# Sliding-window attention with a star-ReLU layer: attention times V in 64x64 tiles, grouped with the scores

## The chip, the cores and the metric

The kernel runs on one core of a Trainium2 chip. The metric is device time in microseconds (us), and the median of a kernel's runs is what counts. A core has TensorE (PE; its weight loads are shown as PEld), VectorE (DVE), ScalarE (ACT), GpSimd (POOL) and SyncE (SP), which issues most transfers. They run side by side and wait for one another by semaphores. TensorE reads SBUF and writes PSUM, which has eight banks of 2 KB in each of 128 partitions.

## The reference

Eight sequences of 576 tokens with 8 heads of 64 go through attention with a window of 32 tokens to either side, and then through a two-layer network.

```python
scores = scale * np.matmul(q, k.transpose(0, 1, 3, 2))       # q, k, v: (8, 8, 576, 64), float32
mask = np.abs(pos[:, None] - pos[None, :]) <= 32
scores = np.where(mask, scores, -1000000000.0)
scores = scores - np.max(scores, axis=-1, keepdims=True)
attn = np.exp(scores)
attn = attn / (np.sum(attn, axis=-1, keepdims=True) + 1e-09)
x = np.matmul(attn, v)                                       # -> 4608 tokens x 512
h = x @ w_in                                                 # 512 x 2048
r = np.maximum(h, 0.0)
g = s * (r * r) + b
out = g @ w_out                                              # 2048 x 512
```

## The kernel before

**Tiles.** The 4,608 tokens, all sequences end to end, are cut into 36 token tiles j of 128. A tile's queries are two halves u of 64. Half 0 sees the 128 keys that begin 32 tokens ahead of the tile, half 1 the 128 keys that begin 64 tokens later. So an attention tile needs 192 keys, which is why k and v are loaded shifted by 32 tokens: load j of k or v holds tokens 128j-32 to 128j+96, and tile j reads loads j and j+1.

**Attention of one tile (`attend`).** SyncE loads q, k and v in rows of 256 bytes (64 floats of a head). GpSimd casts them to bf16 (`KQN`, with k and q of a step side by side, and `VE` for v). `kq_turn` transposes k and q: up to step 11 by eight TensorE transposes into the bank TP and a copy (`kqt<-tp`), later by a DMA transpose. `scores` (line 761) is 24 matmuls in a 64x64 tiling, 16 of 64 columns and 8 of 128, into two banks SC, one for each head of a pair. For each head VectorE then adds the mask and takes the row maximum (line 773), and ScalarE takes the exponential and its row sum (line 781). VectorE inverts the sums, GpSimd multiplies (line 797). P is transposed, from tile 6 on by a DMA transpose (`pts<-p`). `av` (line 845) multiplies with v into the bank AV: 16 matmuls in a 128x64 tiling, 8 with `VE` for half 0 and 8 with `VO` for half 1. `VO` is v shifted by 64 rows, so that half 1's 128 keys stand in one tile of partitions: its two halves are cast by VectorE or ScalarE from two loads (`make_vo`, `vo<-v`). Tiles 0 to 3 use `VE` alone, in two steps and two tilings (`NSPLIT`), tiles 0 to 2 another form of attention altogether (`attend_light`). VectorE copies AV into `XT` (`xt<-av`).

**The two layers.** For a token tile (eight of 128 tokens, then fourteen of 256) the first layer (line 950) is blocks of eight or sixteen matmuls that fill one bank of 512 columns; the banks HT0 and HT1 and, from tile 11 on, TP take turns. ScalarE applies the relu (line 959), VectorE squares into `GT` (line 978). The second layer (line 998) goes by sub-tiles of 128 tokens: 16 matmuls of 512 columns, in four blocks of four, into the bank OUTP or PTP in turn. In the last three token tiles SC1 and AV join in. VectorE scales the bank, adds a constant (line 1012, `outs<-...`), and SyncE stores it.

**The order.** Nothing is ordered by hand. Every step is a node with an engine (or a choice of engines), a cost, a key, and the tiles it reads and writes. `_Plan.order` simulates the engines when the program is built: whichever engine is free first takes, of its nodes that are ready, the one with the smallest key. The result is a fixed instruction order for each engine. A key is about the token number at which the step is due: attention of tile j has 128j less 500 to 640, a first-layer block its token plus its share of the tile, a second-layer block one token tile later; relus, squares and evictions have lower keys. Two nodes that use the same bank or buffer are ordered by that. `PE_SLACK` lets TensorE plan with 400 ns more than the simulated end of another engine's step.

```python
            n = min(here, key=lambda m: (m.key, m.nid))                       # 144
            free[e] = t + n.cost                                              # 157
                    late = PE_SLACK if u.eng == "pe" and t > STEADY else 0.0   # 173
```

**Loads.** `FIRST` lists the loads of the start (K, Q: a whole sequence; i, o: quarters of the two weight matrices; k, q, v: single loads). Later ones come `AHEAD` = 4 tiles ahead, and behind the transposed P of five tiles back (`GATE`).

Of the kernel before, what the change touches and what calls it, by code (L numbers as in the profile page):

```python
# [6 lines left out]
F32 = mybir.dt.float32  # L7
# [18 lines left out]
PE_SLACK, STEADY = 400.0, 60000.0  # L26
FILL, FILL_MIN, FILL_SHARE, FILL_NS = ("attn", "ffn", "sums"), 300.0, 0.7, 115.0


class _Node:  # L30
# [4 lines left out]
                 "hard")  # L35

    def __init__(self, nid, eng, fn, cost, lat, key, dsem, ndma, dtime):
        self.nid = nid
        self.eng = eng
        self.fn = fn  # L40
        self.cost = cost
        self.lat = lat
        self.key = key
        self.deps = {}
        self.dsem = dsem
        self.ndma = ndma
        self.dtime = dtime
# [10 lines left out]
        self.hard = None  # L58


class _Plan:
# [39 lines left out]
    def order(self):  # L101
# [28 lines left out]
        while len(out) < len(self.nodes):  # L130
# [13 lines left out]
            n = min(here, key=lambda m: (m.key, m.nid))  # L144
            if isinstance(n.eng, tuple):
# [11 lines left out]
            free[e] = t + n.cost  # L157
            if n.dsem is None:
# [90 lines left out]
    stage = None  # L249


def bass_sliding_window_symmetric__then__act_starrelu_kernel(
# [20 lines left out]
    FINE, NFLEX, TAIL = 0, 6, 3  # L273
# [8 lines left out]
    NSPLIT, NWHOLE = 4, 0  # L282
# [14 lines left out]
    with ExitStack() as es:  # L297
# [10 lines left out]
        NL, NB, NVE, NVO, NKT, NP, NS, NPT, NG, NR1, NO, NM = 4, 4, 5, 4, 5, 4, 4, 3, 12, 4, 4, 4  # L308
# [4 lines left out]
        Q32 = [sb((128, DM), F32, "q32") for _ in range(NL)]  # L313
        K32 = [sb((128, DM), F32, "k32") for _ in range(NL + 1)]
        V32 = [sb((128, DM), F32, "v32") for _ in range(NL + 1)]
        KQN = [sb((128, 2 * DM), BF16, "kqn") for _ in range(NB)]
        VE = [sb((128, DM), BF16, "ve") for _ in range(NVE)]
        VO = [sb((128, DM), BF16, "vo") for _ in range(NVO)]
        KQT = [sb((128, 2 * NPAIR, 128), BF16, "kqt") for _ in range(NKT)]
# [145 lines left out]
        def parts(t0):  # L465
            got = []
            lo, hi = max(t0, 0), min(t0 + 128, T)
# [8 lines left out]
        def load(src, t0, dst, name, key, sem, x):  # L476
            pcs = parts(t0)

            def fn(e):
                return [e.dma_start(dst[r:r + n, :].rearrange("p (h d) -> p h d", h=H),  # L480
                                    src[b, :, s0:s0 + n, :].rearrange("h s d -> s h d"))
                        for (b, s0, r, n) in pcs]

            tot = sum(n for (_, _, _, n) in pcs)
            gate = turned.get(x - GATE)
            lastload[0] = add("sp", fn, 640.0 * len(pcs), key, writes=[name], dsem=sem,
                              ndma=len(pcs), dtime=1300.0 * tot / 128, behind=lastload[0],
                              ndesc=8 * tot, after=[gate] if gate and gate.eng == "pe" else [])
# [67 lines left out]

        def load_q(j):
            s_ = j % NL
            load(q, 128 * j, Q32[s_], ("Q32", s_), 128 * j - LEAD - 600, f"dq{s_}", j)

        def cast_q(j):
            s_, d_ = j % NL, (j + 1) % NB
            cast(CSET(j), Q32[s_][:, :], ("Q32", s_), KQN[d_][:, DM:2 * DM],
                 ("QN", d_), ckey("q", j, akey(j) - 200))

        def load_k(j):
            s_ = j % (NL + 1)
            load(k, 128 * j - 32, K32[s_], ("K32", s_), 128 * j - LEAD - 730, f"dk{s_}", j - 1)

        def cast_k(j):  # L570
            s_, d_ = j % (NL + 1), j % NB
            cast(CSET(j - 1), K32[s_][:, :], [("K32", s_)],
                 KQN[d_][:, 0:DM], ("KN", d_), ckey("k", j, akey(j) - 330))

        def load_v(j):
            s_ = j % (NL + 1)
            load(v, 128 * j - 32, V32[s_], ("V32", s_), 128 * j - LEAD - 729, f"dv{s_}", j - 1)
# [6 lines left out]
        def make_vo(j):  # L584
            s_, a, b_ = j % NVO, j % NVE, (j + 1) % NVE
            if j < NSPLIT:
                return
# [8 lines left out]
        def kq_turn(j, n0, n1):  # L596
            kn, kt = j % NB, j % NKT
            key = akey(j) - 128
            if j > KQDMA:
                add("sp", lambda e: [e.dma_start_transpose(KQT[kt][:, :, :], KQN[kn][:, :])],  # L600
                    1300, key + 64, reads=[("KN", kn), ("QN", kn)],
                    writes=[("KT", kt), ("QT", kt)], dsem=f"dkt{kt}", dtime=1600, ndesc=1024)
                return
            names = (["K"] if n0 == 0 else []) + (["Q"] if n1 == 8 else [])
# [6 lines left out]
            add("pe", fn, 60 * (n1 - n0), key, reads=[(x + "N", kn) for x in names] + ["IDENT"],  # L611
                writes=["TP"])
            move(FLEX(j - 1), {"dve": 80 + 76.0 * (n1 - n0), "act": 190 + 106.0 * (n1 - n0)},
                 KQT[kt][:, n0:n1, :], TP[:, n0:n1, :], key, ["TP"], [(x + "T", kt) for x in names])

# [125 lines left out]
        def attend(j):  # L741
            key = akey(j)
            ka, kb = j % NKT, (j + 1) % NKT
            ve, vo = j % NVE, j % NVO
# [5 lines left out]
            kq = turns if whole else [("QT", kb), ("KT", ka), ("KT", kb)]  # L750

            def scores(e):
                for pr in range(NPAIR):
                    for u, kt, x0, x1, y0 in ((0, ka, 0, 128, 0), (1, kb, 0, 64, 128), (1, ka, 64, 128, 64)):
                        for hh in range(2):
                            if whole:
                                qq, kk = qs(j, pr, hh, 64 * u, 64 * u + 64), keys(j, pr, hh, y0, y0 + x1 - x0)
                            else:
                                qq = KQT[kb][64 * hh:64 * hh + 64, NPAIR + pr, 64 * u:64 * u + 64]
                                kk = KQT[kt][64 * hh:64 * hh + 64, pr, x0:x1]  # L760
# [4 lines left out]
            add("pe", scores, 400, key, reads=kq, writes=[("SC", 0), ("SC", 1)])  # L765
# [20 lines left out]
            fine = j < FINE  # L786
            for c0, c1 in ((0, 4), (4, 8)) if fine else ((0, 8),):
                ys = range(c0, c1)
                add("dve", lambda e, c0=c0, c1=c1: e.tensor_scalar(
                    SM[mb][:, c0:c1], SM[mb][:, c0:c1], 1e-9, None, ALU.add),  # L790
                    150, key + 3, reads=[("SM", mb, y) for y in ys], writes=[("SE", mb, c0)])
                add("dve", lambda e, c0=c0, c1=c1: e.reciprocal(RC[mb][:, c0:c1], SM[mb][:, c0:c1]),  # L792
                    180, key + 3, reads=[("SE", mb, c0)] + [("SM", mb, y) for y in ys],
                    writes=[("RC", mb, y) for y in ys])
                for y0 in range(c0, c1, 4):
                    def norm(e, y0=y0):
                        return e.tensor_tensor(  # L797
                            P[pb][:, y0:y0 + 4, :], P[pb][:, y0:y0 + 4, :],
                            RC[mb][:, y0:y0 + 4].unsqueeze(2).broadcast_to([128, 4, 128]), ALU.mult)

                    cost = {"dve": 620.0, "pool": 1000.0}
                    eng = ("dve", "pool") if j < NDIV else "pool"
                    add(eng, norm if eng == "pool" else {x: norm for x in eng},
                        cost["pool"] if eng == "pool" else cost, key - 300,
                        reads=[("P", pb, y) for y in range(y0, y0 + 4)]
                        + [("RC", mb, y) for y in range(y0, y0 + 4)],
                        writes=[("P", pb, y) for y in range(y0, y0 + 4)])

            for part, (c0, c1) in enumerate(((0, 4), (4, 8)) if fine else ((0, 8),)):
                avp, ares = AV, "AV"  # L810
                if fine and part:
                    avp, ares = PTPF[:, :].rearrange("p (a b) -> p a b", b=128), "PTP"
                ptp = halves(PTPF if fine and part else AVF)

                if j >= PDMA:
                    turned[j] = add("sp", lambda e: [e.dma_start_transpose(
                        PTS[ptb][:, :, :], P[pb][:, :, :].rearrange("p a b -> p (a b)"))],
                        1300, key + 4, reads=[("P", pb, y) for y in range(8)],
                        writes=[("PTS", ptb, y) for y in range(8)], dsem=f"dpt{ptb}", dtime=1600, ndesc=1024)
                else:  # L820
                    def turn(e, c0=c0, c1=c1, ptp=ptp):
                        for y in range(c0, c1):
                            r = e.transpose(ptp[:, y, :], P[pb][:, y, :], IDENT[:, :])
                        return r

                    turned[j] = add("pe", turn, 59 * (c1 - c0), key + 4,
                        reads=[("P", pb, y) for y in range(c0, c1)] + ["IDENT"], writes=[ares])
# [251 lines left out]
```

## Time and profile before

| What | Value |
|---|---|
| median of three runs | 326.09 us (325.95 to 326.39) |
| the profiled execution | 325.7 us, span 323.9 us from first to last instruction |
| TensorE clock granted over the span | 0.995 |
| scores, 64x64, line 761 (tiles 4 to 35) | 768 matmuls |
| av, line 845 (tiles 3 to 35) | 280 matmuls from `VE`, 256 from `VO` |
| first layer, 256 columns | 896 matmuls, 273 ns each |
| second layer, 512 columns, OUTP and PTP | 467 matmuls recorded, 379 to 380 ns each |
| casts `vo<-v` | 49 on VectorE (552 ns), 15 on ScalarE (613 ns) |
| `xt<-av` on VectorE | 33 of 686 ns |
| evictions `outs` of 512 columns on VectorE | 744 to 748 ns |
| DMA | 173,121 packets, 61.56 MB, 163,728 packets under 512 bytes |

Matmuls are pipelined: a matmul's time in the profile runs from its start to its result, and the next one starts much earlier. What a block costs TensorE is read from the starts of the blocks. A few matmul records are missing, so a block of four may show as three.

### The profile page before, as it was taken

How to read it: one execution, taken by the hardware profiler on the slowest of the kernel's cores; microseconds unless marked ns; L12 is line 12 of the kernel's file. 1: busy time of each engine (PE TensorE's matmuls, PEld its weight loads, DVE VectorE, ACT ScalarE, POOL GpSimd, SP SyncE). 2: the span in 40 equal slices, each digit the busy share in tenths (PEclk: the TensorE clock that was granted, in tenths of full speed). 3: DMA queues.
4: the chain of work that ended last, by engine and by line, in shares of the span. 5: the costliest groups of instructions: out<-in, count | busy, mean ns of one | idle time of the engine just before them, and what ended most of it. 6: DMA issues, size and time to landing. Idle time of an engine off the chain costs nothing.

```text
span 323.9 us, 10043 instructions
## 1 busy us (share of the span) xinstructions
PE 310.7 (96%) x3877; PEld 214.9 (66%) x3925; DVE 236.1 (73%) x912; ACT 207.7 (64%) x715; POOL 164.6 (51%) x219
## 2 busy tenths in 40 slices
PE   6889989999999999999999999999999999999996
PEld 4557957766776757666675767575767666666664
DVE  2456886989987788894887787879867889843332
ACT  4414854688984859873769865779746778823330
POOL 5567589646767364655464564536671646410000
PEclk9799999999999999999999999999999999999999
DMA  5999879959999999999999999999999564420011
GB/s 168 340 300 263 293 254 233 234 128 232 204 176 212 203 208 191 231 186 241 183 237 215 211 229 219 210 220 213 201 223 215 125 140 99 98 67 34 32 64 68
DMA packets 173121, 61.56 MB, mean 190 GB/s; under 512 B 163728, under 2 KB 163984, under 8 KB 173072
## 3 DMA queue, kind: packets, MB, share of 16 engines
q1 hardware_dynamic: 172784, 60.90, 90.0%
q8 instruction: 31, 0.51, 0.7%
q14 instruction: 18, 0.15, 0.2%
q10 hardware_dynamic: 288, 0.00, 0.0%
HBM read 37.03 MB, written 9.44 MB: 143 GB/s over the span
## 4 chain that ended last, share of the span: by engine, by line
PE 85%; DVE 6%; ACT 3%; DMA 3%; issue 2%; POOL 0%; SPq 0%; POOLq 0%
PE ht L950 28%; PE outp L998 16%; PE ptp L998 15%; PE tp L950 8%; PE sc L761 3%; PE av L845 3%; DMA gt<-in_q_dram 3%; ACT p L781 2%; PE sc L998 2%; DVE gt L978 2%; PE av L998 2%; ACT r L959 1%; PE ht L431 1%; PE av L701 1%; PE tp L608 1%
## 5 line engine op out<-in xcount | busy, mean ns | idle before, releaser
L950 PE MATMUL ht<-xt,win 128*128 128x256 bf16 (+1 forms) x1152 | 113.7, 249 | 0.1
L781 ACT ACTIVATE p<-ss,mx 128x128 bf16<-128x128 f32 x264 | 102.5, 391 | 16.0 <-DVE mx L773 14.8
L978 DVE TENSOR_TENSOR gt<-r 128x512 bf16<-128x512 bf16 x144 | 78.2, 545 | 46.5 <-ACT r L959 45.2
L950 PEld LDWEIGHTS ht<-xt,win 128*128 128x128 bf16 x1152 | 91.2, 98 | 19.0 <-issue 0.3
L797 POOL TENSOR_TENSOR p<-p,rc 128x512 bf16<-128x512 bf16 x65 | 70.4, 1103 | 57.4 <-DVE rc L792 57.4
L959 ACT ACTIVATE r<-ht 128x512 bf16<-128x512 f32 x112 | 66.1, 592 | 44.7 <-PE ht L950 43.0
L998 PE MATMUL outp<-wout,gt 128*128 128x512 bf16 (+1 forms) x245 | 62.4, 373 | 2.5 <-issue 1.4
L773 DVE CUSTOM_DVE_ANT_0 ss<-sc,mask 128x128 f32<-128x128 f32 x264 | 61.5, 280 | 3.6 <-PE sc L761 3.3
L998 PE MATMUL ptp<-wout,gt 128*128 128x512 bf16 x238 | 61.5, 379 | 1.5 <-issue 0.6
L781 ACT ACTIVATION_READ_ACCUMULATOR p<-ss,mx 128x1 f32 x264 | 49.9, 189 | 0.0
L500 POOL CAST ve<-v 128x512 bf16<-128x512 f32 x37 | 24.9, 675 | 31.8 <-PE av L845 30.4
L998 PEld LDWEIGHTS ptp<-wout,gt 128*128 128x128 bf16 x256 | 24.0, 98 | 22.6
L998 PEld LDWEIGHTS outp<-wout,gt 128*128 128x128 bf16 x272 | 24.3, 98 | 18.6 <-DVE gt L978 0.2
L950 PE MATMUL tp<-xt,win 128*128 128x256 bf16 x256 | 33.2, 273 | 0.0
L959 ACT ACTIVATE r<-tp 128x512 bf16<-128x512 f32 x32 | 19.0, 595 | 20.1 <-PE tp L950 18.9
L500 POOL CAST kqn<-k 128x512 bf16<-128x512 f32 x33 | 22.4, 679 | 15.8 <-DMA k<-in_k_dram 15.8
L950 PEld LDWEIGHTS tp<-xt,win 128*128 128x128 bf16 x256 | 24.8, 98 | 6.1
L500 DVE CAST vo<-v 64x512 bf16<-64x512 f32 x49 | 27.1, 552 | 0.9
L500 DVE CAST xt<-av 128x512 bf16<-128x512 f32 x33 | 22.6, 686 | 6.0 <-PE av L845 5.8
L500 POOL CAST kqn<-q 128x512 bf16<-128x512 f32 x32 | 22.2, 693 | 2.2 <-DMA q<-in_q_dram 2.1
L773 DVE DVE_READ_ACCUMULATOR2_ANT mx<- 128x1 f32 x264 | 21.1, 80 | 0.0
L761 PEld LDWEIGHTS sc<-kqt 64*64 64x64 bf16 x768 | 10.7, 108 | 9.0 <-issue 6.8
(125 smaller groups left out, 255.1 us busy)
## 6 DMA issues: line engine op xcount, KB each, us to landing
out_dram<-outs SPq DMA_DIRECT2D x35, 256.0 KB, 3.1
v<-in_v_dram SPq DMA_DIRECT2D x28, 256.0 KB, 5.3
q<-in_q_dram SPq DMA_DIRECT2D x28, 256.0 KB, 4.4
k<-in_k_dram SPq DMA_DIRECT2D x25, 256.0 KB, 3.9
gt<-in_moe_w_in_dram SPq DMA_DIRECT2D x4, 1024.0 KB, 10.1
gt<-in_moe_w_out_dram SPq DMA_DIRECT2D x4, 1024.0 KB, 5.7
v<-in_v_dram SPq DMA_DIRECT2D x8, 192.0 KB, 4.6
k<-in_k_dram SPq DMA_DIRECT2D x7, 192.0 KB, 3.2
```

Of the source, the lines that this page charges most:

```text
L431: r = e.matmul((HT[1] if stage == "attn" else OUTP)[:, 0:256], lhsT=ONES[:, 0:128], rhs=ONES[:, :], start=True, stop=True)
L500: return e.tensor_copy(dst, src)
L608: r = e.transpose(TP[:, pr, :], KQN[kn][:, 128 * pr:128 * pr + 128], IDENT[:, :])
L761: r = e.matmul(SC[hh][64 * u:64 * u + 64, pr, x0:x1], lhsT=qq, rhs=kk, start=True, stop=True)
L773: lambda e, ss=ss, x=x, y=y, pr=pr, hh=hh: e.tensor_tensor_reduce(out=SS[ss][:, x, :], in0=SC[hh][:, pr, :], in1=MASK[kind][:, :], scale=- ...
L781: lambda e, ss=ss, x=x, y=y: e.activation(P[pb][:, y, :], SS[ss][:, x, :], AF.Exp, bias=MX[mb][:, y:y + 1], scale=-1.0, accum_out=SM[mb][: ...
L797: return e.tensor_tensor(P[pb][:, y0:y0 + 4, :], P[pb][:, y0:y0 + 4, :], RC[mb][:, y0:y0 + 4].unsqueeze(2).broadcast_to([128, 4, 128]), AL ...
L845: r = e.matmul(avp[64 * hh:64 * hh + 64, pr, 64 * u:64 * u + 64], lhsT=vt[k0:k1, d0:d0 + 64], rhs=PTS[ptb][k0:k1, 2 * pr + hh, 64 * u:64 * ...
L950: r = e.matmul(hbank[:, nt * f:nt * f + nt], lhsT=WIN[:, kc, 128 * ft:128 * ft + 128], rhs=XT[:, kc, x0:x0 + nt], start=(kc == 0), stop=(k ...
L959: return e.activation(R1[rb][:, :], hbank[:, :], AF.Relu, bias=0.0, scale=1.0)
L978: return e.tensor_tensor(d, r, r, ALU.mult)
L998: r = e.matmul(op_[:, 0:cn], lhsT=GT[:, g_, fc, :], rhs=WOUT[:, fc, c0:c0 + cn], start=(fc == 0), stop=(fc == 15))
```

## The change

1. **AV in 64x64 tiles.** From tile 6 (`NOLD`) on, AV is 24 matmuls. Eight take rows 64 to 127 of `VE[j]` (the 64 keys that all 128 queries of the tile use) with 128 columns into the bank PTP. Sixteen take rows 0 to 63 of `VE[j]` for half 0 and of `VE[j+1]` for half 1, with 64 columns, into the bank AV. ScalarE copies PTP into `HALF`, and VectorE adds AV and `HALF` into `XT`. `VO` is no longer made there. Tiles 3 to 5 use the old form with `VO`, in one group of 16.
2. **Grouping.** Nodes have a mode; `scores` and the new AV are "small". In the planner each change of mode on TensorE costs 97 ns (`CHANGE`). In small mode another ready small node is taken next, if its key is less than 800 (`HOLD`) above the one due. In full mode a single ready small node that is due is put off, as long as a full one is ready with a key less than 200 (`DEFER`) above.
3. **k in 512-byte rows.** k is loaded in chunks of 256 tokens, with two tokens in a partition (partition p has tokens 2p and 2p+1), which is 512 bytes in one piece. q keeps its rows and is put together in chunks of two tiles. k and q are cast, transposed and buffered apart, by chunks. The scores read the keys of a transposed chunk as pairs: a token of one plane, then one of the other, 1,024 bytes apart. `FIRST` has k2 for k4 and k5, and q5 ahead of v5.
4. **One output bank.** From token 640 (`ONE` = 5 tiles) on, up to the last three token tiles, all second-layer sub-tiles use OUTP, since PTP is AV's second bank.

```diff
+HOLD, DEFER, CHANGE = 800.0, 200.0, 97.0
...
             n = min(here, key=lambda m: (m.key, m.nid))
+            if e == "pe":
+                small = [m for m in here if m.mode == "small"]
+                if self.mode == "small" and n.mode != "small" and small:
+                    m = min(small, key=lambda m: (m.key, m.nid))
+                    if m.key < n.key + HOLD:
+                        n = m
+                elif self.mode != "small" and len(small) == 1 and n is small[0]:
+                    full = [m for m in here if m.mode != "small"]
+                    if full:
+                        m = min(full, key=lambda m: (m.key, m.nid))
+                        if m.key < n.key + DEFER:
+                            n = m
...
             free[e] = t + n.cost
+            if e == "pe":
+                if n.mode != self.mode:
+                    free[e] += CHANGE
+                self.mode = n.mode
...
-    FIRST = "K0 K1 Q0 Q1 v0 v1 i0 i1 i2 v2 v3 i3 v4 k4 k5 q4 o0 o1|v5 o2 o3||||"
+    FIRST = "K0 K1 Q0 Q1 v0 v1 i0 i1 i2 v2 v3 i3 v4 k2 q4 o0 o1|q5 v5 o2 o3||||"
...
+    AVK, NOLD, ONE, NVO = 5, 6, 5, 2
...
+        NR, NKT = {"k": 2, "q": 2}, {"k": 3, "q": 2}
...
+        def load_k(c):
+            s_ = c % NR["k"]
+            load("k", 256 * c - 32, 256, 2, R32["k"][s_], ("R32", "k", s_, 0), 2 * c - 1,
+                 256 * c - LEAD - 730, f"dk{s_}")
...
+        def cast_kq(x, c):
+            j = 2 * c - (x == "k")
+            src, dst = R32[x][c % NR[x]], KQN[x][c % NB]
+            if x == "k":
+                src = src[:, :].rearrange("p (h t d) -> p t h d", h=H, t=2)
+                dst = dst[:, :].rearrange("p (t h d) -> p t h d", h=H, t=2)
...
             if j > KQDMA:
-                add("sp", lambda e: [e.dma_start_transpose(KQT[kt][:, :, :], KQN[kn][:, :])],
+                add("sp", lambda e: [e.dma_start_transpose(flat, kn[:, :])],
...
             def fn(e):
-                for pr in range(n0, n1):
-                    r = e.transpose(TP[:, pr, :], KQN[kn][:, 128 * pr:128 * pr + 128], IDENT[:, :])
+                for i in range(8):
+                    r = e.transpose(TP[:, i, :], kn[:, 128 * i:128 * i + 128], IDENT[:, :])
                 return r
...
-                                kk = KQT[kt][64 * hh:64 * hh + 64, pr, x0:x1]
+                                rows, p0 = slice(64 * hh, 64 * hh + 64), 64 * (j % 2) + y0 // 2
+                                qq = KQT["q"][c % NKT["q"]][rows, j % 2, pr, 64 * u:64 * u + 64]
+                                kk = KQT["k"][(c + p0 // 128) % NKT["k"]][
+                                    rows, :, pr, p0 % 128:p0 % 128 + (x1 - x0) // 2].rearrange(
+                                    "q t p -> q p t")
...
-            add("pe", scores, 400, key, reads=kq, writes=[("SC", 0), ("SC", 1)])
+            add("pe", scores, 265, key, reads=kq, writes=[("SC", 0), ("SC", 1)]).mode = "small"
...
+            def av(e):
+                for pr in range(NPAIR):
+                    for hh in range(2):
+                        d0, y = 128 * pr + 64 * hh, 2 * pr + hh
+                        e.matmul(PTPF[64 * hh:64 * hh + 64, 128 * pr:128 * pr + 128],
+                                 lhsT=VE[ve][64:128, d0:d0 + 64], rhs=PTS[ptb][64:128, y, :],
+                                 start=(pr == 0), stop=(pr == NPAIR - 1))
+                    for u in range(2):
+                        for hh in range(2):
+                            d0, y = 128 * pr + 64 * hh, 2 * pr + hh
+                            r = e.matmul(AV[64 * hh:64 * hh + 64, pr, 64 * u:64 * u + 64],
+                                         lhsT=VE[(j + u) % NVE][0:64, d0:d0 + 64],
+                                         rhs=PTS[ptb][0:64, y, 64 * u:64 * u + 64],
+                                         start=(pr == 0 and u == 0),
+                                         stop=(pr == NPAIR - 1 and u == 1))
+                return r
+
+            add("pe", av, 265, key + AVK, reads=pts + [("VE", ve), ("VE", (j + 1) % NVE)], writes=["AV", "PTP"]).mode = "small"
+            hb = j % 2
+            add("act", lambda e: e.copy(HALF[hb][:, :], PTPF[:, :]), 620, key + AVK, reads=["PTP"],
+                writes=[("HALF", hb)])
+            add("dve", lambda e: e.tensor_tensor(
+                XT[:, :, 128 * (j % NX):128 * (j % NX) + 128], AV[:, :, :],
+                HALF[hb][:, :].rearrange("p (a b) -> p a b", b=128), ALU.add), 690, key + 5,
+                reads=["AV", ("HALF", hb)], writes=[("XT", j % NX, x) for x in range(2)])
...
-                                 )[ocnt[0] % (4 if last else 2)]
+                                 )[ocnt[0] % (4 if last else 2 if t0 < 128 * ONE else 1)]
```

More of the change, by code (lines that the diff above doesn't have):

```diff
@@ L58, in __init__ @@
         self.hard = None
+        self.mode = "full"
 class _Plan:
@@ L249 @@
     stage = None
+    mode = "full"
 def bass_sliding_window_symmetric__then__act_starrelu_kernel(
@@ new lines, in attend, with turn @@
+            pts = [("PTS", ptb, y) for y in range(8)]
+            if j >= PDMA:
+                turned[j] = add("sp", lambda e: [e.dma_start_transpose(
+                    PTS[ptb][:, :, :], P[pb][:, :, :].rearrange("p a b -> p (a b)"))],
+                    1300, key + 4, reads=[("P", pb, y) for y in range(8)],
+                    writes=pts, dsem=f"dpt{ptb}", dtime=1600, ndesc=1024)
+            else:
+                ptp = halves(AVF)
+                def turn(e):
+                    for y in range(8):
+                        r = e.transpose(ptp[:, y, :], P[pb][:, y, :], IDENT[:, :])
+                    return r
+                turned[j] = add("pe", turn, 472, key + 4,
+                    reads=[("P", pb, y) for y in range(8)] + ["IDENT"], writes=["AV"])
+                move(("act", "dve"), {"act": 1040.0, "dve": 810.0}, PTS[ptb][:, :, :], ptp, key + 4,
+                     ["AV"], pts)
@@ new lines, in attend, with av_one @@
+            if j < NOLD:
+                vo = j % NVO
+                def av_one(e):
+                    for u, vt in ((0, VE[ve]), (1, VO[vo])):
+                        for y in range(8):
+                            pr, hh = y // 2, y % 2
+                            r = e.matmul(AV[64 * hh:64 * hh + 64, pr, 64 * u:64 * u + 64],
+                                         lhsT=vt[:, 64 * y:64 * y + 64],
+                                         rhs=PTS[ptb][:, y, 64 * u:64 * u + 64],
+                                         start=(u == 0 and pr == 0), stop=(u == 1 and pr == 3))
+                    return r
+                add("pe", av_one, 460, key + AVK,
+                    reads=pts + [("VE", ve), ("VO", vo, 0), ("VO", vo, 64)], writes=["AV"])
+                add("dve", lambda e: e.tensor_copy(
+                    XT[:, :, 128 * (j % NX):128 * (j % NX) + 128], AV[:, :, :]), 690, key + 5,
+                    reads=["AV"], writes=[("XT", j % NX, x) for x in range(2)])
+                return
@@ L922, in attention_until @@
                 if NL <= x < NT:
-                    for what in (f"k{x + 1}", f"q{x}", f"v{x + 1}"):
+                    for what in ([f"k{x // 2 + 1}"] if x % 2 else []) + [f"q{x}", f"v{x + 1}"]:
                         if what not in place:
```

206 lines of the change are left out of this document (78 added, 128 removed).

## The prediction

> **What bounds the kernel now.** I read the page first: its busy times, its slices, then its chain of waits. Of this profiled execution (325.7 us, span 323.9 us) TensorE is busy 96%, and 85% of the chain that ended last runs through it.
>
> ```profile
> PE 310.7 (96%) x3877; PEld 214.9 (66%) x3925; DVE 236.1 (73%) x912; ACT 207.7 (64%) x715; POOL 164.6 (51%) x219
> PE   6889989999999999999999999999999999999996
> PE 85%; DVE 6%; ACT 3%; DMA 3%; issue 2%; POOL 0%; SPq 0%; POOLq 0%
> ```
>
> A busy share can hide stalls, so I asked next for TensorE's waits from 47 us to 320 us. No wait there is longer than 0.2 us, and those put down to "issue" are slots whose first matmul record is missing (three records of four). From 47 us on TensorE always has the next instruction, and what is taken from its stream comes off the end. The price of the pieces is read from the timeline of TensorE in a steady stretch (start, length, what):
>
> ```profile
> 158.23 1.03 PE L998 MATMUL outp<-wout,gt 128*128 128x512 bf16 x4
> 159.09 1.03 PE L998 MATMUL ptp<-wout,gt 128*128 128x512 bf16 x4
> 160.05 0.45 PE L761 MATMUL sc<-kqt 64*64 64x128 bf16 x24
> 160.43 1.04 PE L998 MATMUL outp<-wout,gt 128*128 128x512 bf16 x4
> 161.40 0.32 PE L845 MATMUL av<-pts,ve 128*64 128x64 bf16 x8
> ...
> 171.92 0.32 PE L845 MATMUL av<-pts,ve 128*64 128x64 bf16 x8
> 172.07 0.29 PE L845 MATMUL av<-pts,vo 128*64 128x64 bf16 x8
> 172.29 0.45 PE L761 MATMUL sc<-kqt 64*64 64x128 bf16 x24
> ```
>
> The reader is to look at starts. Four 512-wide matmuls take 158.23 to 159.09, 0.86 us. The four from 159.09 should end at 159.95; the scores start at 160.05: 0.10 us lost where the tiling goes from 128x128 to 64x64. The 24 score matmuls have all started 0.25 us later (0.45 less the 0.19 to 0.2 of the last), so they need 0.265 us, yet the next block starts only at 160.43, after 0.38. So a lone score block costs 0.48 us: 0.265 of work and 0.215 for the two changes of tiling. A lone AV block (16 matmuls of 128x64) costs 0.10 + 0.37 = 0.47. At 171.92 AV and scores adjoin, and one entry, 0.10, is saved; I count 5 such pairs among the 30 scores and 30 AVs of token tiles 6 to 35.
>
> **AV and grouping.** Before, those 60 blocks cost 30 x 0.48 + 30 x 0.47 - 5 x 0.10 = 28.0 us. After, AV is 24 matmuls in 64x64, eight of 128 columns and sixteen of 64, the same counts and widths as scores, on two banks as scores are. Nearest row: 0.265 us. From below, 512 columns on each of four quadrants, 0.216 us by the 512-wide matmul; from above, 24 at the old AV's 14 ns a start (8 starts in 0.10 to 0.12), 0.336. I take 0.265; the upper end adds 30 x 0.07 = 2.1 us. Each run of small blocks, however long, then costs 0.215 more: 60 x 0.265 + R x 0.215 = 15.9 + 0.215 R for R runs. All alone (R = 60): 28.8, 0.8 us worse. All paired (R = 30): 22.35. The planner holds a single ready small block back for up to 200 keys, at 128 keys per token tile and about 7.9 us a tile some 12 us; in the trace the next small block comes 1 to 7 us later. So pairs should be the rule, with singles where no full block is ready: R = 34, 23.2 us, **-4.8 us**.
>
> **Transposes by TensorE.** k and q are now turned in groups of eight for nine chunks up to tile 11: 72 instead of 60 (the row `tp<-ident,kqn` x60). Eight take 0.61 us less the last one's 0.22, so 56 ns each: **+0.7 us**, on the stall-free path.
>
> **The old AV of tiles 3 to 5.** Tile 3 loses its split (two groups, at 45.27 and 46.73, with a full block between): one entry and exit less and eight matmuls less, **-0.3 us**. It gains two half casts on VectorE or ScalarE (0.55, 0.61 us) ahead of it. TensorE waited 0.98 us there for VectorE's copy of P, so if the casts get in front of that, up to 1.1 us is lost; I take nothing, as they depend on loads only.
>
> **One output bank after token 640.** 25 sub-tiles of second-layer work (tiles 5 to 29) must wait for VectorE to empty the bank before. From the end of the issue of the last matmul: 0.16 us of pipeline, a median wait of 0.15, the eviction's 0.745, some 0.1 for the semaphore: 1.15 us, at worst (VectorE was late by 1.0 to 1.2 three times) about 2.2. It is hidden by first-layer blocks of 0.87 us, two of which are enough, and three banks feed them; before, bursts of three are common. Floor 0, ceiling 25 x 1.15 = 29 us. Near the floor, since first-layer work equals second-layer work and can run ahead: five evictions uncovered by 0.16, **+0.8 us**.
>
> **Beside the path.** ScalarE gains 30 copies PTP to HALF (the relu row of the same shape: 0.595 each, 17.9 us) and loses up to 15 V casts (9.2); it was busy 70 to 74% of 100 to 290 us. VectorE loses most of 49 V casts of 0.552 (27.1 us); its xt copy (0.686) becomes an add, 0.692 by the `xn` row. But this add now waits for ScalarE's HALF, and behind it in VectorE's queue stand squares, score reductions and the output evictions. TensorE hides that as long as the bank's 1.15 us is hidden. GpSimd casts the same elements. SyncE issues one k load where there were two, and 24 turns of k and q instead of 25; k's packets double from 256 to 512 bytes and halve in number. 2,048 packets go, 1,024 stay, so k's packet time cannot rise if a packet less than doubles; 256-byte packets took some 23 ns each in the trace, 2,048-byte ones about 95. In the start list k2 stands for k4 and k5, and q5 passes v5, o2 and o3: a shorter k against one more load, within 1 us either way, taken as nothing.
>
> **Scores from paired k rows.** k's turned chunk holds even tokens in one plane and odd ones in another, so scores stream their moving operand from two places 1,024 bytes apart in turn. No row shows TensorE reading so. ScalarE's `kwt<-tp` copies out of PSUM step 1,024 bytes and take 586 to 591 ns, against 592 for a plain relu, so stepping cost nothing there. Below: nothing (a gain is excluded, the columns are the same). Above: half rate, 0.216 us more a block. I take nothing, the nearest row.
>
> [...]
>
> **Sum.** -4.8 + 0.7 - 0.3 + 0.8 = -3.6 us: 322.1 for the profiled execution, whose 325.7 lies 0.4 under the median of 326.1; against that median, **322.5 us**. Its own range: R from 30 to 42 (-0.9, +1.7), bank 0 to 1.6, start +-1: 319.8 to 325.4.
>
> **Rivals.** *Slower by the strided k.* If the stream halves, 32 score blocks (tiles 4 to 35) cost 0.216 more: +6.9, 329.4 us. It decides above 3.6 / 32 = 0.11 us a block. For it: nothing in the trace excludes it. Against: the PSUM row. 0.17.
> *The single bank.* If the planner cannot place two first-layer blocks after each sub-tile, or the add on VectorE holds evictions back, each of 25 costs up to 1.15. At a third of that, +8.8 more: 331; from 0.18 us a sub-tile the gain is gone. Against: squares and relus kept three banks turning without a stall. 0.09.
> *Grouping does not happen.* R near 55, as with 5 pairs now: 15.9 + 11.8 = 27.7, so -0.3 + 0.7 - 0.3 + 0.8: 327.0, just slower. 0.05.
> *More than pairs.* With P turned early, runs of three: R = 22, -7.4, and the start a little shorter by VectorE's relief: 318.5. 0.09.
> *The forecast:* 0.60.
>
> **Numbers.** A measurement can tell about 0.2%, 0.65 us, from no change. Faster: forecast 0.58 of its 0.60, runs of three 0.09, and the mild ends of the bank and the strided k, 0.04: 0.71. Same 0.05, slower 0.24. Range 318.5 to 329.4: it reaches runs of three and the strided k; the bank's bad end stays out.
>
> **What would show it.** Right: in TensorE's timeline AV as `64*64 x24` beside scores, about 34 runs after 62 us, 0.265 us from a block's first start to the next block's, one exit of 0.115 a run; no TensorE wait on `outs` over 0.2 us; `half<-ptp` about 0.6. Wrong: score blocks of 0.48 inside (strided k); gaps ahead of `outp` released by VectorE (one bank); lone AV blocks (no grouping); waits on DMA or SP before 62 us (start list).

## The result, and the profile after

The changed kernel takes **330.96 us** (median of four runs, 330.83 to 332.44), the kernel before 326.02 (325.88 to 326.39) beside it: a ratio of 1.016 (95% interval 1.013 to 1.019). It is slower by some 5 us, where 3.6 us less was forecast, and it lies just above the range. The profiled execution took 331.0 us, 5.3 more than that of before; its span is 329.3 us. Medians and ranges here leave out executions with a lower granted clock that came out over 1.5% above the fastest of their kernel.

The page of the changed kernel, in the parts that were shown of before:

```profile
PE 314.1 (95%) x4119; PEld 220.5 (67%) x4169; DVE 219.6 (67%) x869; ACT 215.9 (66%) x731; POOL 163.1 (50%) x220
PE   6889999999999999999999999999999999999996
PE 79%; DMA 9%; DVE 3%; POOL 3%; issue 3%; SPq 2%; POOLq 0%
...
L901 ACT COPY half<-ptp 128x512 f32<-128x512 f32 x30 | 17.4, 579 | 10.5 <-PE av L892 10.5
...
L903 DVE TENSOR_TENSOR xt<-av,half 128x512 bf16<-128x512 f32 x30 | 20.5, 683 | 1.1 <-ACT half L901 1.1
```

TensorE is as busy as before in every slice, and VectorE has lost 16 us of work. So the 5 us are no new idle time in the middle of the kernel. TensorE's waits from 47 to 324 us (us in total, times, longest) say the same; those put down to "issue" are again slots whose first record is missing:

```profile
PE outp L1040 <- issue: 4.0, 25, 0.2
PE ht L992 <- DVE xt L903: 0.4, 1, 0.4
PE tp L929 <- DVE clo L925: 0.2, 1, 0.2
PE ptp L886 <- DMA pts<-p: 0.2, 1, 0.2
```

No wait on `outs` is left, and hardly one of any kind. The work itself takes longer. TensorE's timeline (start, length, what) shows which, in three places: scores alone, AV alone, AV and scores together.

```profile
126.96 1.04 PE L992 MATMUL ht<-xt,win 128*128 128x256 bf16 x8
127.93 0.69 PE L798 MATMUL sc<-kt,qt 64*64 64x128 bf16 x24
128.55 0.61 PE L1040 MATMUL outp<-wout,gt 128*128 128x512 bf16 x2
...
153.57 0.24 PE L886 MATMUL ptp<-pts,ve 64*64 64x128 bf16 x2
153.58 0.25 PE L892 MATMUL av<-pts,ve 64*64 64x64 bf16 x4
...
153.95 1.04 PE L1040 MATMUL outp<-wout,gt 128*128 128x512 bf16 x4
...
213.46 0.24 PE L886 MATMUL ptp<-pts,ve 64*64 64x128 bf16 x2
...
213.74 0.66 PE L798 MATMUL sc<-kt,qt 64*64 64x128 bf16 x22
214.33 1.05 PE L992 MATMUL ht<-xt,win 128*128 128x256 bf16 x8
```

The reader is to compare starts again. Scores alone hold TensorE from 127.93 to 128.55, **0.62 us, where they held it 0.38 before**. The new AV, with the same counts and widths in the same tiling, takes 153.57 to 153.95, 0.38. The pair takes 0.87. The entry (127.93 less 126.96 and 0.87) is 0.10, as before. To the nanosecond, a score block alone has grown from 0.377 to 0.620 us, by 0.243. The two kinds of block differ in what they stream: AV reads P in one piece, the scores read k as pairs from two planes.

### The profile page after: what moved, and what is told of

The parts are those of the page before. It is cut to its first block, busy times and chain, and to the rows that moved or that the text cites. A ratio compares the mean times of both kernels' runs of the same rounds, so it can differ in the third digit from the quotient of the medians.

```text
span 329.3 us, 10479 instructions
## 1 busy us (share of the span) xinstructions
PE 314.1 (95%) x4119; PEld 220.5 (67%) x4169; DVE 219.6 (67%) x869; ACT 215.9 (66%) x731; POOL 163.1 (50%) x220
## 4 chain that ended last, share of the span: by engine, by line
PE 79%; DMA 9%; DVE 3%; POOL 3%; issue 3%; SPq 2%; POOLq 0%
PE outp L1040 26%; PE ht L992 25%; PE tp L992 8%; PE sc L798 5%; DMA gt<-in_q_dram 3%; DMA v<-in_v_dram 2%; PE sc L1040 2%; DMA pts<-p 2%; DMA r32k<-in_k_dram 2%; PE ptp L886 2%; PE ptp L1040 2%; PE av L1040 2%; DVE gt L1020 1%; SPq L506 1%; POOL p L831 1%
## 5 line engine op out<-in xcount | busy, mean ns | idle before, releaser
L1020 DVE TENSOR_TENSOR gt<-r 128x512 bf16<-128x512 bf16 x144 | 82.4, 574 | 54.8 <-ACT r L1001 53.5
L1040 PE MATMUL outp<-wout,gt 128*128 128x512 bf16 (+1 forms) x436 | 111.9, 375 | 5.1 <-issue 4.1
L1040 PEld LDWEIGHTS outp<-wout,gt 128*128 128x128 bf16 x480 | 43.4, 98 | 33.8 <-issue 0.4
L526 POOL CAST kn<-r32k 128x512 bf16<-128x512 f32 x34 | 21.5, 659 | 7.3 <-DMA r32k<-in_k_dram 7.3
L1054 DVE SCALAR_TENSOR_TENSOR outs<-outp,scb,cvec 128x512 f32<-128x512 f32 (+1 forms) x30 | 22.1, 736 | 3.4 <-PE outp L1040 3.4
L901 ACT COPY half<-ptp 128x512 f32<-128x512 f32 x30 | 17.4, 579 | 10.5 <-PE av L892 10.5
L526 POOL CAST qn<-r32q 128x512 bf16<-128x512 f32 x32 | 20.1, 628 | 4.2 <-DMA r32q<-in_q_dram 4.2
L798 PE MATMUL sc<-kt,qt 64*64 64x64 bf16 (+1 forms) x768 | 22.1, 243 | 0.0
L903 DVE TENSOR_TENSOR xt<-av,half 128x512 bf16<-128x512 f32 x30 | 20.5, 683 | 1.1 <-ACT half L901 1.1
L798 PEld LDWEIGHTS sc<-kt,qt 64*64 64x64 bf16 x768 | 17.5, 107 | 4.7 <-issue 3.6
```

Of the source, the lines that this page charges most:

```text
L526: return e.tensor_copy(dst, src)
L798: r = e.matmul(SC[hh][64 * u:64 * u + 64, pr, x0:x1], lhsT=qq, rhs=kk, start=True, stop=True)
L901: add("act", lambda e: e.copy(HALF[hb][:, :], PTPF[:, :]), 620, key + AVK, reads=["PTP"], writes=[("HALF", hb)])
L903: add("dve", lambda e: e.tensor_tensor(XT[:, :, 128 * (j % NX):128 * (j % NX) + 128], AV[:, :, :], HALF[hb][:, :].rearrange("p (a b) -> p ...
L1020: return e.tensor_tensor(d, r, r, ALU.mult)
L1040: r = e.matmul(op_[:, 0:cn], lhsT=GT[:, g_, fc, :], rhs=WOUT[:, fc, c0:c0 + cn], start=(fc == 0), stop=(fc == 15))
```

## The experiments

The expectations name theories by letters. S is that the strided read of k is what costs; B is that the cause lies around the score blocks, above all in the single output bank. W, L, P, C and H are explained where they come.

**The strided read alone, in the kernel before.** Two planes of the buffer that holds k and q take turns, for tiles 5 to 35, and the scores also wait for the second plane; nothing else changes. What it computes are no longer the reference's scores.

```diff
-                                kk = KQT[kt][64 * hh:64 * hh + 64, pr, x0:x1]
+                                n, g = (x1 - x0) // 2, RUN[j % 4]                    # RUN = (1, 1, 1, 1)
+                                kk = (... if j == WHOLE else
+                                      KQT[kt][64 * hh:64 * hh + 64, pr:pr + 5:4, x0 // 2:x0 // 2 + n].rearrange(
+                                          "q t (p g) -> q p t g", g=g))
```

> The kernel before, and only the moving operand of its scores changed: from tile 5 on it is read as pairs from two places 1,024 bytes apart (one element of the k plane, one of the q plane, so the scores are not those of the reference). Theory S (the strided read alone makes the score blocks longer): a block's last matmul starts 0.47 us after its first instead of 0.25, the block takes 0.63 instead of 0.38, and 31 blocks give +7.8 us: 333.8. Theory B (the blocks of the changed kernel are long because of what stands around them, such as the single output bank or the AV in the same tiling): unchanged, 326.0, blocks of 0.38.

Measured: 333.81 us (333.73 to 334.23) against 326.02, ratio 1.0236 (1.0222 to 1.0249), +7.8. The timeline of this kernel:

```profile
157.26 0.69 PE L765 MATMUL sc<-kqt 64*64 64x128 bf16 x24
157.88 1.05 PE L954 MATMUL ht<-xt,win 128*128 128x256 bf16 x8
```

The block is the same 0.62 us long, and from 47 to 324 us TensorE shows no wait over 0.15 us. Theory S holds, size and place: 31 blocks of 0.243 are 7.5. There is neither a single output bank nor a new AV in this kernel, so theory B falls as the cause of the long blocks.

**How long a run must be.** The same edit, with 1, 2, 4 and 8 elements in one piece before the plane changes, by tile.

```diff
-    RUN = (1, 1, 1, 1)
+    RUN = (1, 2, 4, 8)
```

> The same as the strided kernel before, but the length of the runs that are read in one piece is 1, 2, 4 and 8 elements by tile modulo 4 (the scores are not those of the reference). Theory S in its form 'a single element at each place is what costs': 0.63 us for runs of one and 0.38 for runs of two, four and eight; about 328. In its form 'each change of place costs': 0.63, 0.50, 0.44, 0.41; about 329.7. Theory B: all 0.38, 326.

Measured once: 328.17 us. Its timeline has the four kinds in turn, 1, 2, 4, 8:

```profile
132.73 0.69 PE L765 MATMUL sc<-kqt 64*64 64x128 bf16 x24
133.35 1.04 PE L1002 MATMUL outp<-wout,gt 128*128 128x512 bf16 x4
...
140.01 0.47 PE L765 MATMUL sc<-kqt 64*64 64x128 bf16 x24
140.42 1.05 PE L954 MATMUL ht<-xt,win 128*128 128x256 bf16 x8
...
154.51 0.45 PE L765 MATMUL sc<-kqt 64*64 64x128 bf16 x24
154.89 1.05 PE L954 MATMUL ht<-xt,win 128*128 128x256 bf16 x8
...
161.55 0.45 PE L765 MATMUL sc<-kqt 64*64 64x128 bf16 x24
161.93 1.04 PE L1002 MATMUL outp<-wout,gt 128*128 128x512 bf16 x4
```

0.62, 0.41, 0.38, 0.38 us. Only a single element at each place comes near to halving the rate (first to last start 0.467 us against 0.252); two in a piece nearly restore it (0.276), four do. The distance between the planes is the same in all, so it is the run that counts. Of the two forms of theory S the first, that a single element is what costs, is right but for this small price of pairs, which took a tenth longer than runs of four.

**One output bank alone, in the kernel before.**

```diff
-                                 )[ocnt[0] % (4 if last else 2)]
+                                 )[ocnt[0] % (4 if last else 2 if t0 < 640 else 1)]
```

> The kernel before, with one output bank from token 640 on as in the changed kernel. Theory S: the bank costs no more than the few waits seen after the change, 326 to 327. Theory B: the bank costs what the change lost, 329 to 331, with gaps ahead of the second-layer blocks released by VectorE.

Measured: 329.24 us (328.31 to 329.52), ratio 1.0088 (1.0073 to 1.0103), +3.2. TensorE's waits, 47 to 324 us, of this kernel:

```profile
PE outp L998 <- DVE outs L1012: 2.0, 2, 1.2
PE ht L950 <- DVE mx L773: 0.3, 1, 0.3
```

Two waits for an eviction, at 101 and 119 us, are 2.0 of the 3.2. The time is theory B's, and yet this is not what slowed the changed kernel, whose own waits show no eviction at all. Its order is another one. That its slower scores leave VectorE more room is not the reason: repaired, with quick scores and the one bank, it shows no wait for an eviction either (two experiments on).

**The change with k loaded as before**, in two loads of 128 tokens, so that a plane holds tokens in order and the scores read in one piece.

```diff
-            load("k", 256 * c - 32, 256, 2, R32["k"][s_], ("R32", "k", s_, 0), 2 * c - 1, ...
+            for t in range(2):
+                if 256 * c - 32 + 128 * t < T:
+                    load("k", 256 * c - 32 + 128 * t, 128, 1, R32["k"][s_][:, DM * t:DM * t + DM], ...
...
-                                    rows, :, pr, p0 % 128:p0 % 128 + (x1 - x0) // 2].rearrange("q t p -> q p t")
+                                    rows, p0 % 256 // 128, pr, p0 % 128:p0 % 128 + x1 - x0]
```

> The changed kernel, with k loaded in 256-byte rows, a chunk as two planes of 128 tokens in order, so that scores read their keys in one piece; grouping, AV in 64x64 and the one bank stay. Theory S: score blocks of 0.38, 32 x 0.25 us less: 323.0. Theory B: 330 to 331. If k's 512-byte rows are needed for the transfers to keep up: score blocks of 0.38, but waits on DMA, 325 or more.

Measured: 327.51 us (325.99 to 328.42), ratio 1.004 (1.0023 to 1.0057). The blocks are back at 0.252 us first to last start, but the time is 4.5 above theory S. In this order there are 48 runs of small blocks instead of 40 (1.7 us), and TensorE waits 1.0 us once for the transposed P. It waits nowhere for k, so the longer rows were not needed for the transfers to keep up.

**The change with k in 512-byte rows but read in runs of 32.** The scores come out with a block's even tokens ahead of its odd ones; the masks are permuted to match, and ScalarE writes its exponentials back in the old order.

```diff
-                                    "q t p -> q p t")
+                                    "q t (b p) -> q b t p", p=32)
...
-                            P[pb][:, y, :], SS[ss][:, x, :], AF.Exp, bias=MX[mb][:, y:y + 1],
+                            P[pb][:, y, :].rearrange("q (b p t) -> q b t p", b=2, t=2),
+                            SS[ss][:, x, :].rearrange("q (b t p) -> q b t p", b=2, t=2), AF.Exp, ...
```

> The changed kernel with its 512-byte k rows, but scores read their keys in runs of 32 (even tokens, then odd tokens of a block of 64), with the mask in that order; ScalarE writes the exponentials back in token order. TensorE's order has the same 40 runs of small blocks. Theory S (the strided read is the loss, all else near the forecast): score blocks of 0.252 from first to last start, 32 x 0.25 = 8.0 us less: 323.0. Theory W (the order and its waits, above all of the one bank, are a second loss of some us, as the kernel before with one bank was 3.2 us slower): 324.5 to 326. If ScalarE's scattered write costs, its exponentials are over 0.39 us.

Measured: 326.01 us (324.39 to 327.09), ratio 0.9995 (0.9977 to 1.0014). The pair of AV and scores now takes 0.63 us instead of 0.87, and the number of runs is 40 as in the change:

```profile
134.92 0.24 PE L896 MATMUL ptp<-pts,ve 64*64 64x128 bf16 x2
...
135.55 1.04 PE L1050 MATMUL outp<-wout,gt 128*128 128x512 bf16 x4
```

But 5.0 of the 7.8 us came back, not all: the time is at the upper end of theory W. TensorE's waits of this kernel, 47 to 324 us:

```profile
PE ptp L896 <- DMA pts<-p: 0.9, 2, 0.5
PE ht L1002 <- DVE xt L913: 0.8, 2, 0.5
PE sc L804 <- DMA qt<-qn: 0.6, 1, 0.6
PE tp L939 <- DVE clo L935: 0.2, 1, 0.2
```

They are 2.5 us, against 0.8 (without the "issue" ones) in the change. TensorE, faster, has caught up with what feeds it: transposed P, q, and `XT`. None of the waits is for an eviction from the one bank, which theory W had named first. ScalarE's strided write has its price too, in the page's row of exponentials (0.429 us against 0.392):

```profile
L825 ACT ACTIVATE p<-ss,mx 128x128 bf16<-128x128 f32 x264 | 107.4, 429 | 13.9 <-DVE mx L816 13.5
```

**The same without the grouping.**

```diff
-            if e == "pe":        # the block that prefers or puts off a small node
+            if False:
```

> The same, without the planner's HOLD and DEFER rules (the price of a change of tiling stays): 56 runs of small blocks instead of 40. Theory 'a run costs 0.215': 16 x 0.215 = 3.4 us slower than with grouping. Rival (grouping also delays blocks, which costs as much): the same time within 1 us.

Measured: 330.26 us (329.57 to 333.55), ratio 1.015 (1.0112 to 1.0188), 4.25 above the kernel with grouping, with 56 runs instead of 40. Sixteen runs by 0.215 would be 3.4. TensorE's waits are 4.2 us here (among them 1.4 for a cast of q) against 2.5 with grouping, and may be the rest. The grouping gains about what the forecast's price of a run says.

**The same with two output banks throughout** (`ONE` = 99, so sub-tiles and AV share PTP).

```diff
-    AVK, NOLD, ONE, NVO = 5, 6, 5, 2
+    AVK, NOLD, ONE, NVO = 5, 6, 99, 2
```

> As e5, but second-layer sub-tiles keep taking OUTP and PTP in turn, so that AV and the second layer share PTP; the planner then puts small blocks together by three and four, 23 runs. Theory W: 17 runs less at 0.215 and the waits on the one bank gone, -3.7 to -5 against e5. Rival (AV waits for PTP to be emptied, and attention falls behind): slower than e5, with TensorE idle ahead of AV or of first-layer blocks that wait for xt.

Measured: 400.17 us, ratio 1.2265 (1.2243 to 1.2287). Only 23 runs are left, but the bank is now the bound. The largest of TensorE's waits, 47 to 324 us:

```profile
PE ptp L896 <- DVE xt L913: 14.6, 9, 2.2
PE ht L1002 <- DVE xt L913: 10.9, 7, 2.0
```

AV waits until the tile before has left the banks, and the first layer then waits for `XT`. The granted clock over the span was 0.919, against 0.995 before, so part of the loss is a slower TensorE (last section). AV's second bank can't be shared with the outputs in this way.

**The same, holding a single small block back longer.**

```diff
-HOLD, DEFER, CHANGE = 800.0, 200.0, 97.0
+HOLD, DEFER, CHANGE = 800.0, 800.0, 97.0
```

> As e5, with DEFER 800 instead of 200: a lone small block is held back longer, 36 runs instead of 40. Theory 'a run costs 0.215': -0.9 us against e5. Rival (held blocks come late): the same or slower, with waits on xt.

Measured: 334.15 us (331.82 to 334.67), ratio 1.0232 (1.0203 to 1.0261). Four runs fewer (36), 0.9 us by the forecast's price, and new waits that cost far more, these three ahead:

```profile
PE sc L804 <- DVE mx L816: 2.1, 2, 1.7
PE ptp L896 <- DMA pts<-p: 1.7, 3, 1.1
PE av L879 <- DVE pts L527: 1.4, 1, 1.4
```

**Parts 1, 2 and 4 in the kernel before, with its k and q.** The planner's block, `new_av` and the one bank are the change's; loads, casts and turns are those of before.

```diff
-            if j < NSPLIT:
+            if j < NSPLIT or j >= NOLD:                                    # no VO
...
+                if j >= NOLD:
+                    new_av(j, key, ptb, ve)                                # AV, HALF and the add as in the change
+                    continue
...
-                                 )[ocnt[0] % (4 if last else 2)]
+                                 )[ocnt[0] % (4 if last else 2 if t0 < 128 * ONE else 1)]   # ONE = 5
```

> The kernel before with parts 1, 2 and 4 of the change (AV in 64x64 on two banks, grouping, one output bank) and without part 3: k and q are loaded, cast and transposed as before. 46 runs of small blocks from tile 6 on instead of 55 before. By the ledger of blocks -2.2 us for the runs and blocks. Theory C (the waits that came with the changed kernel belong to the chunks of 256 tokens): no more than 0.5 us of waits, 324. Theory W (they belong to the one bank and to AV's longer chain over HALF): 2 to 3 us of waits, 326 to 327.

Measured: 329.29 us (327.01 to 331.11), ratio 1.0101 (1.0064 to 1.0137). That is 2 us above the dearer of the two theories, and which waits make it up is not known. But the chunks of k show no sign of being a burden: with them, read in runs of 32, the kernel takes 326.0, without them some 3 us more, of which six more runs would be 1.3.

**The same, holding back up to 400 keys.**

```diff
-HOLD, DEFER, CHANGE = 800.0, 200.0, 97.0
+HOLD, DEFER, CHANGE = 800.0, 400.0, 97.0
```

> As e9, with DEFER 400 instead of 200: 35 runs instead of 46, so 2.4 us less in changes of tiling. Theory 'runs decide': 2 us faster than e9. Theory H (a block held back lets the attention behind it come late, as with DEFER 800): slower than e9, with TensorE waiting on xt, pts or the score maxima.

Measured: 332.46 us (331.25 to 332.77), ratio 1.0189 (1.0168 to 1.021). As in the other kernel, holding back costs more than it saves. The timeline shows a second price:

```profile
103.22 0.24 PE L894 MATMUL ptp<-pts,ve 64*64 64x128 bf16 x2 [0.97 <-DMA pts<-p]
...
104.64 0.45 PE L782 MATMUL sc<-kqt 64*64 64x128 bf16 x24 [0.97 <-DVE mx L794]
106.65 3.59 PE L1004 MATMUL ht<-xt,win 128*128 128x256 bf16 x16 [1.56 <-DVE xt L912]
```

After three waits (in brackets) of 0.97, 0.97 and 1.56 us close together, sixteen matmuls take 3.59 us. At their usual 0.109 us a start it would be 1.9.

**AV's second bank taken from the first layer** (TP) instead of from the outputs, which keep two banks.

```diff
-                        e.matmul(PTPF[64 * hh:64 * hh + 64, 128 * pr:128 * pr + 128],
+                        e.matmul(TPF[64 * hh:64 * hh + 64, 128 * pr:128 * pr + 128],
...
-                hb, rb = hcnt[0] % (3 if KQDMA < NT and t0 >= 128 * KQDMA else 2), rcnt[0] % NR1
+                hb, rb = hcnt[0] % 2, rcnt[0] % NR1
```

> As e9, but AV's second bank is TP, and the second layer keeps OUTP and PTP in turn; the first layer then has two banks instead of three from tile 11 on. 52 runs. Theory W: without the one bank no waits on evictions; but two first-layer banks make TensorE wait for the relu, up to 0.3 us for each of some 90 blocks. If second-layer blocks fill those gaps: 325; if not: 330 or more, with waits released by ScalarE's r.

Measured: 373.11 us, ratio 1.1437 (1.1413 to 1.1462). AV waits five times for the transposed P, 22.3 us together. Why the order comes out so badly was not followed further; as a way to a second output bank it fails.

**One output bank from token 1,280 on, in the kernel before**: does it cost at one place only, or all along?

```diff
-                                 )[ocnt[0] % (4 if last else 2)]
+                                 )[ocnt[0] % (4 if last else 2 if t0 < 1280 else 1)]
```

> The kernel before, with one output bank from token 1,280 on instead of 640 (e3: 329.2). Theory L (the one bank costs only while attention builds its lead, before some 120 us): 326 to 326.5, no wait on an eviction over 0.3 us. Theory P (it costs all along): 328 to 329, with waits later.

Measured: 329.86 us (328.48 to 330.14), ratio 1.0114 (1.0095 to 1.0134), +3.9. TensorE's waits for an eviction:

```profile
PE outp L998 <- DVE outs L1012: 2.2, 4, 1.0
```

They have moved, to 134 to 180 us, and add up to some 2 us again. Theory P holds: the bank costs in this kernel wherever it begins.

**The new AV later, in the kernel that reads k in runs of 32**: from tile 12, one bank from tile 10.

```diff
-    AVK, NOLD, ONE, NVO = 5, 6, 5, 2
+    AVK, NOLD, ONE, NVO = 5, 12, 10, 2
```

> As e5 (512-byte k rows read in whole runs), but the new AV starts at tile 12 instead of 6 and the one bank at token 1,280 instead of 640. Some 46 runs of blocks from tile 6 on, 1.3 us more than in e5. Theory L: the waits between 95 and 120 us go, 3 us less: 324. Theory P: 327.

Measured: 325.37 us (324.39 to 326.38) against 326.0, ratio 0.9981 (0.9966 to 0.9997). It lies 0.2% below the kernel before, and its interval just excludes no change. It falls between the two theories: the wait on P's transpose is gone from its list, as theory L had it, but others stand in its place (0.7 us for an eviction, 1.1 for a cast of q).

**The same, from tile 16** (`NOLD` = 16, `ONE` = 13).

> The same with tile 16 and token 1,664. Theory L: no more to gain, and fewer tiles with the new AV: 324 to 324.5. Theory P: 326 to 327.

Measured: 325.27 us (323.93 to 328.07), ratio 0.9984 (0.9963 to 1.0005): no further gain that can be told.

## Why the prediction was wrong

**The step that failed: "I take nothing, the nearest row."** The scores' read of paired k rows was costed at nothing because ScalarE's stepped copy out of PSUM cost nothing. That row belongs to another engine with another memory, whose copy takes 0.59 us for 512 columns; it says nothing on TensorE, which takes a 512-wide matmul in 0.216. It isn't the same step either: by the code (`turn_raw`) that copy steps 64 float32 elements, 256 bytes and not 1,024. The first rival had the mechanism, and nearly its size: 0.216 a block was forecast there, 0.243 measured, 7.8 us over 32 blocks instead of 6.9. Of the 0.243, 0.215 lie between a block's first and last start, as the rival had it, the rest after the last start. A chance of 0.17 was low for a read that no row of TensorE showed. The halving, and so the +6.9, was an estimate that no run had shown; the runs then showed 0.467 us from a block's first start to its last, where 0.252 had been.

Put together, after less before, from the profiled executions (the rows for the transposes and the old AV are worked out from counts and prices of blocks, the waits from how much later than usual a matmul starts):

| Term | Forecast | Measured | From |
|---|---|---|---|
| AV and grouping | -4.8 | -3.9 | 20 pairs of 0.73 and 20 single blocks of 0.475 (with entry), read in one piece, against 28.0 |
| transposes of k and q | +0.7 | +0.7 | 72 instead of 60, below |
| old AV of tiles 3 to 5 | -0.3 | about -0.3 | no longer in two groups |
| one output bank | +0.8 | 0 | no wait on `outs` |
| scores from paired rows | 0 | +7.8 | 32 x 0.243 |
| other waits | 0 | about +1.0 | `ht` on `xt` at 223 us, AV on P's transpose at 98.5 us, one at 117 us |
| sum | -3.6 | +5.3 | 5.3 between the two executions |

**AV and grouping: right in kind, the number of runs too low.** Each AV block costs what a score block did before, as forecast, and the grouping is worth 4.25 us when it alone is taken away from the repaired kernel. But 40 runs remain, 20 of them pairs, where R = 34 was taken (the range had 30 to 42). By the forecast's 0.215 that is 1.3 us of the -4.8; by the starts, 0.9.

**Transposes: right.** The timings of bank TP's matmuls in the changed kernel have 40 of k and 32 of q (duration min, median, max in ns, first and last start):

```profile
L642 PE MATMUL tp<-ident,kn x40: 219/219/230, 39.8 to 89.3; 128*128 128x128 bf16 x40
...
L642 PE MATMUL tp<-ident,qn x32: 219/219/230, 45.3 to 86.2; 128*128 128x128 bf16 x32
```

**One output bank: right in the change, wrong as a price of its own.** Five uncovered evictions were put at 0.8 us; none shows. Taken alone it costs 3.2 or 3.9 us. So the cover that the forecast named, first-layer blocks that run ahead, is there in some orders and not in others. It is there in the changed kernel and, with quick scores, in the repaired one; in the kernel before it is not. What in the order decides that was not followed up.

**Beside the path: right.** In the changed kernel the copy to `HALF` took 0.579 us (0.595 forecast), the add 0.683 (0.692); neither holds TensorE up by more than 0.4 us.

**Two slips in the sums.** The forecast's own range, R, bank and start added, ends at 326.0 and not at 325.4. The runs of three come to 319.9 by the terms given, so their 318.5 asks more of the start than the 1 us allowed for it. Neither changes the sign of the forecast.

**What the sum had not seen.** With 7.8 us for the read and 40 runs, the forecast would have been 331.6, close to the 330.96 measured. That it is so close owes something to luck: the 0.8 us for the bank, which did not come, stand for the 1.0 of waits that no term had. And the reverse does not hold: with the read repaired the kernel is not at 323 but at 326.0. The stream of TensorE had been free of waits at the pace of before. Made 5 us faster, it meets P's transposes, q's transposes and `XT`; the single bank shows only in its neighbours (0.2 to 0.8 us). The waits have grown by 1.7 us, and some 1 us of the gap stays unaccounted for. How far the one bank, by the order that it forces, or the longer way from AV to `XT` (copy, then add) is behind these waits stays open: in both kernels that kept two output banks throughout AV shared its second one with other work, and lost far more.

## What to carry to other kernels

Price a changed access pattern on the engine that reads it and from the memory it reads; where no row shows that, measure one block first, and keep TensorE's moving operand in runs of at least two, better four, bf16 elements, the lengths that were enough here (24 starts in 0.276 and 0.252 us, against 0.467 for single elements). Changes of tiling can be counted as runs, at about 0.22 us each here, but there is a limit to holding a block back to save one: up to 200 keys gained 4.25 us in one kernel, and up to 400 or 800, in two kernels, lost more in waits than the saved runs were worth. A stream without waits has only as much margin as nobody has used: before a gain on it is booked in full, ask which of its feeders is late next.

## What the runs showed of the hardware that was not expected

- In the kernel before with the strided read, where each bf16 element of the scores' moving operand lay alone (planes 1,024 bytes apart), TensorE took it at little more than half rate: 24 score matmuls had all started after 0.467 us instead of 0.252. Two elements in a piece: 0.276. Four or eight: 0.252.
- In the kernel before with the new AV and `DEFER` 400, three waits of 0.97 to 1.56 us between 102 and 106.7 us were followed by some 5 us in which 256-wide matmuls started every 0.214 us instead of 0.109. The granted clock of that kernel (fortieths of the span) falls there too, in the thirteenth slice and the one after:

```profile
PEclk9799999999998799999999999999999999999999
```

Single waits of 0.9 to 1.0 us later in the same kernel (at 123, 151 and 167 us) were not followed by such a stretch. In the kernel with two output banks throughout it comes back every 22 us or so: twelve times, two waits of 1.0 to 2.1 us close together are followed by 2 to 6 us in which 256-wide matmuls start every 0.213 us. The granted clock over its span was 0.919, against 0.995 before.
